# New tables for the order, the engines and the idle products of an mLSTM kernel with a dense layer on one core

## The chip, the cores and the metric

One core of one Trainium2 chip runs the whole program. The metric is the device time of one execution in microseconds (us). Three executions of the kernel before are given, and a profile of one more.

## The reference

The first part is a recurrent attention (mLSTM) over B = 4 sequences, H = 8 heads, 768 steps and a head width of 40, with gates i, f and o. Its result, turned into 3072 tokens of 320 numbers, goes through a dense layer with a softplus between two products:

```
C = f_stab * C + i_stab * outer(v_t, k_t)
n = f_stab * n + i_stab * k_t
y_t = o * (C q_t) / max(|n . q_t|, 1)
...
h = x @ w_in                                   # 320 -> 2048
g = max(h, 0) + log1p(exp(-|h|))
out = g @ w_out                                # 2048 -> 320
```

f_stab and i_stab come from the gates and their running maximum m.

## The kernel before

**Steps and tiles.** A step is 128 time steps of one sequence with all eight heads; it is named by sequence and chunk, and 0_0 is the first chunk of sequence 0. ORDER (line 40) takes the steps 1_0, 2_0, 0_0, then 3_0, 0_1, 0_2 and so on. Three steps make a tile of 384 tokens, and there are eight tiles. The layer can start on a tile when the three steps are done, so tile 0 consists of 1_0, 2_0 and 0_0.

**A step.** `load` (L402, L405) brings q, k and v. `decay` runs a scan on DVE (L432) for the decays pw and a product gw (L437). `plain_scores` multiplies k by q on PE (L483). `by_decays` (L513, DVE) multiplies the scores by the decays. `states` (L500, PE) forms v times k from the scaled values vw (`scaled`, L446 or L450), and `keep_states` copies the result out of PSUM into cp (copy, L789). `values` reads the old states (L599) and the scores (L607) on PE. `sum_values` takes them on DVE (y1z at L446, yy at L628), `norm` forms the denominator nq (L636, L637), `scale_gate` multiplies the out gate og by it (L641), `gated` forms x (L653, on POOL), `turn_x` turns x on PE (L736), and `high_x` and `low_x` (L789, L746) split it into two parts of X. Step states wait for `by_decays` of the same step, because both use one pair of PSUM banks.

**Gates.** `first_gates` (L168 to L198) serves the first chunks, `later_gates` (L208 to L253) the rest: gc at L218 is a subtraction, L220 an exponential, L223, L225 and L226 set up d, and L231 scans. L764 and L768 load and squash the out gates; L843 loads an activation table.

**Weights.** They come as 64-bit words and are made into floats on the chip, in eight slices of w_in (wr, wih, wil) and eight of w_out (wo, woh, wol). `single` has the steps mag (L273 on ACT, L275 elsewhere), the low half (L279), the high half (L283) and a join on DVE into sgi or sgo (L287). `weights` then casts the rounded part into wih (L789) and subtracts it for the remainder (L325 for the wide part wil, L327 for the short third slice); `weights_out` does the same for woh (L789) and wol (L335).

**The layer.** A block is 128 of the 2048 inner columns of one tile: eight products hp (L1003), softplus on ACT (L890, L891), a remainder on DVE (L894), nine products po (L966). The blocks go in the order tile 0 blocks 0 to 9, tile 1 blocks 0 to 15, tile 0 blocks 10 to 15 (SPLIT = 10), then tiles 2 to 7.

**What sets the order.** All work beside the products is a set of generators in a heap. WHEN (L1060) gives each piece of work, by name, a time counted in products of the layer; those below zero come before the first. `tick` runs all pieces due by the current product, `wait_for` runs as many as a product needs, and every engine executes its instructions in the order in which they were recorded. PICK (L1109) names the engine of an elementwise operation: V is DVE, A is ACT, G is POOL; where it has no entry, the default at the call of `pick` holds. WARM (L1108) is the number of identity products that `keep_warm` (L758) puts on PE at eleven places. They write to a corner of PSUM that nobody reads.

```
    def at_of(name, at, base=0):
        return base + WHEN[name] if name in WHEN else at
...
    def pick(name, default):
        return engines[PICK.get(name, default)]
...
    def keep_warm(k):
        for i in range(k):
            nc.tensor.matmul(wm, ident, ident, start=True, stop=True)
```

Of the kernel before, what the change touches and what calls it, by code (L numbers as in the profile page):

```python
# [44 lines left out]
def mlstm_moe_kernel(  # L45
# [20 lines left out]
    p1 = ctx.enter_context(tc.tile_pool(name="p1", bufs=1))  # L66
    p2 = ctx.enter_context(tc.tile_pool(name="p2", bufs=2))
# [692 lines left out]
    og = p2.tile([128, NH, DM], F32, tag="X", bufs=XB, name="og")  # L760
# [296 lines left out]
    def finished(t):  # L1057
        return all(s in ended for s in range(t * NG, (t + 1) * NG))

    WHEN = {'l0': -300, 'p0': -299, 'p1': -298, 'l1': -297, 'p2': -296, 'wl0': -295, 'j0': -294, 'k0': -293, 'p3': -292,  # L1060
# [47 lines left out]
    WARM = {0: 8, 1: 0, 2: 2, 3: 1, 4: 2, 5: 0, 6: 1, 7: 4, 8: 0, 9: 3, 10: 1}  # L1108
# [106 lines left out]
```

## Time and profile before

| what | us |
|---|---|
| three executions | 438.61, 432.89, 437.66 |
| their median | 437.66 |
| the profiled execution | 433.22 |
| its span in the profile | 431.4 |
| PE busy in the span | 419.5 (97%) |
| DVE, ACT, POOL busy | 254.2, 214.7, 106.8 |

Times in the profile count from the start of the span. The profiled execution is 1.8 us longer than its span; that part lies around it. Its granted TensorE clock was 0.991 of full speed on the mean. In the rows, a duration stands behind the start, `x8` is a number of instructions of one kind taken together, and a bracket like [0.56 <-ACT cp] is the time that the engine stood idle before, and what ended it. The operand names drop their buffer numbers. A tile that a step reads under several names (pa, po) is a PSUM bank that was reused.

### The profile page before, as it was taken

How to read it: one execution, taken by the hardware profiler on the slowest of the kernel's cores; microseconds unless marked ns; L12 is line 12 of the kernel's file. 1: busy time of each engine (PE TensorE's matmuls, PEld its weight loads, DVE VectorE, ACT ScalarE, POOL GpSimd, SP SyncE). 2: the span in 40 equal slices, each digit the busy share in tenths (PEclk: the TensorE clock that was granted, in tenths of full speed). 3: DMA queues.
4: the chain of work that ended last, by engine and by line, in shares of the span. 5: the costliest groups of instructions: out<-in, count | busy, mean ns of one | idle time of the engine just before them, and what ended most of it. 6: DMA issues, size and time to landing. Idle time of an engine off the chain costs nothing.

```text
span 431.4 us, 12677 instructions
## 1 busy us (share of the span) xinstructions
PE 419.5 (97%) x5284; PEld 408.0 (95%) x5284; DVE 254.2 (59%) x479; ACT 214.7 (50%) x445; POOL 106.8 (25%) x171
## 2 busy tenths in 40 slices
PE   7769999999999999999999999999999999999996
PEld 7669989999999999999999999999999999999996
DVE  6889998767866646565646556456465555422221
ACT  5688998476455333644336333634236433333332
POOL 3643436444454212212312311222222200000000
PEclk9969999999999999999999999999999999999999
DMA  7888895864655363435273273344363330001001
GB/s 193 265 268 248 252 256 162 248 176 121 157 160 155 117 148 108 130 97 161 67 200 112 64 176 99 112 125 127 98 192 107 71 89 28 2 0 48 0 2 46
DMA packets 52089, 55.93 MB, mean 130 GB/s; under 512 B 5664, under 2 KB 42176, under 8 KB 52032
## 3 DMA queue, kind: packets, MB, share of 16 engines
q1 hardware_dynamic: 49008, 51.68, 43.6%
q10 hardware_dynamic: 3024, 3.44, 2.3%
q8 instruction: 41, 0.67, 0.7%
q14 instruction: 16, 0.13, 0.1%
HBM read 46.47 MB, written 8.64 MB: 128 GB/s over the span
## 4 chain that ended last, share of the span: by engine, by line
PE 93%; DMA 3%; DVE 1%; ACT 1%; POOL 1%; issue 0%; SPq 0%; POOLq 0%; DVEq 0%; ACTq 0%
PE hp L1003 41%; PE po L966 40%; PE hp L483 3%; PE pa L667 2%; PE pa L679 2%; DMA qk<-in_qk 2%; PE hp L500 1%; DMA wr<-in_w_in 1%; PE po L758 1%; PE pa L500 1%; POOL x L653 1%; PE pa L599 1%; PE pa L607 0%; PE pa L483 0%; PE pa L156 0%
## 5 line engine op out<-in xcount | busy, mean ns | idle before, releaser
L1003 PE MATMUL hp<-X,wih 128*128 128x384 f32 x768 | 175.8, 338 | 0.3 <-DVE gl L894 0.3
L890 ACT ACTIVATE gh<-hp 128x384 fp32r<-128x384 f32 x128 | 62.8, 491 | 166.7 <-PE hp L1003 139.0
L894 DVE TENSOR_TENSOR gl<-hp,gh 128x384 fp32r<-128x384 f32 x128 | 70.6, 554 | 123.6 <-ACT hp L891 123.4
L1003 PEld LDWEIGHTS hp<-X,wih 128*128 128x128 f32 x768 | 133.3, 188 | 0.9 <-DVE gl L894 0.6
L966 PE MATMUL po<-woh,gl 128*128 128x320 f32 x384 | 83.2, 313 | 0.0
L966 PE MATMUL po<-wol,gh 128*128 128x320 f32 x384 | 80.8, 310 | 0.0
L966 PE MATMUL po<-woh,gh 128*128 128x320 f32 x384 | 80.7, 310 | 0.1
L966 PEld LDWEIGHTS po<-woh,gh 128*128 128x128 f32 x384 | 65.8, 188 | 0.5 <-ACT woh L789 0.4
L1003 PE MATMUL hp<-X,wil 128*128 128x384 f32 x256 | 65.8, 338 | 0.0
L966 PEld LDWEIGHTS po<-woh,gl 128*128 128x128 f32 x384 | 62.3, 188 | 0.9
L966 PEld LDWEIGHTS po<-wol,gh 128*128 128x128 f32 x384 | 62.0, 188 | 0.6
L891 ACT ACTIVATE hp<-hp 128x384 f32<-128x384 f32 x128 | 62.4, 488 | 0.0
L446 POOL TENSOR_TENSOR vw<-vt,gw 128x328 f32<-128x328 f32 x22 | 17.3, 788 | 118.0 <-DVE gw L437 109.8
L1003 PEld LDWEIGHTS hp<-X,wil 128*128 128x128 f32 x256 | 46.1, 188 | 0.2
L446 POOL TENSOR_TENSOR values_in<-vt,gT 128x328 f32<-128x328 f32 x18 | 13.3, 737 | 65.2 <-PE pa L679 58.6
L432 DVE TENSOR_TENSOR_SCAN pw<-fb,ident 128x512 f32<-128x512 f32 x21 | 26.5, 1263 | 0.0
L578 POOL TENSOR_TENSOR c<-c,cp 104x164 f32<-104x164 f32 x20 | 14.5, 725 | 14.6 <-DMA fc_d<-d 8.2
L713 DVE RECIPROCAL nm<-nm 128x128 f32<-128x128 f32 x18 | 17.2, 953 | 0.6
L511 DVE TENSOR_TENSOR pw<-hp,pw 128x256 f32<-128x256 f32 x36 | 13.6, 419 | 4.6 <-PE hp L500 4.1
L789 ACT COPY cp<-hp 104x164 f32<-104x164 f32 (+1 forms) x31 | 8.2, 283 | 16.2 <-DVE pw L511 14.3
L446 POOL TENSOR_TENSOR c<-c,flast 104x164 f32<-104x164 f32 x33 | 15.5, 470 | 1.0
L569 POOL TENSOR_TENSOR c<-c,cp 104x164 f32<-104x164 f32 x20 | 13.1, 656 | 9.9 <-ACT cp L789 8.2
(162 smaller groups left out, 428.5 us busy)
## 6 DMA issues: line engine op xcount, KB each, us to landing
vt<-in_vk SPq DMA_DIRECT2D x24, 324.0 KB
qk<-in_qk SPq DMA_DIRECT2D x48, 160.0 KB
fb<-fz_d SPq DMA_DIRECT2D x42, 128.0 KB
wo<-in_w_out SPq DMA_DIRECT2D x8, 640.0 KB
wr<-in_w_in SPq DMA_DIRECT2D x8, 512.0 KB
eg<-in_oT SPq DMA_DIRECT2D x6, 576.0 KB
yd<-y SPq DMA_DIRECT2D x36, 96.0 KB
out<-ob ACTq DMA_DIRECT2D x21, 160.0 KB
```

The lines of the kernel that those rows point to most:

```text
L432: nc.vector.tensor_tensor_scan(z.pw.rearrange(flat), z.fb.rearrange(flat), ident4.rearrange(flat), 0.0, ALU.mult, ALU.add)
L446: e.tensor_tensor(to, of, by.unsqueeze(3).broadcast_to([to.shape[0], a, b, w]), op=ALU.mult)
L483: nc.tensor.matmul(z.ga[x][y * Q : (y + 1) * Q, (i * NQ + q) * Q : (i * NQ + q + 1) * Q], z.k[rows, g, ts], z.q[rows, g, ts], start=True, ...
L511: nc.vector.tensor_tensor(pw[:, x], z.ga[x][:, 0:CP0], pw[:, x], op=ALU.mult)
L569: nc.gpsimd.tensor_tensor(heads(z.cm), heads(z.cm), z.cp[:, :, 0], op=ALU.add)
L578: nc.gpsimd.tensor_tensor(heads(c), heads(c), z.cp[:, :, 1], op=ALU.add)
L713: nc.vector.reciprocal(nm, nm)
L890: nc.scalar.activation(gh, hp, AF.Softplus)
L891: nc.scalar.activation(hp, hp, AF.Softplus)
L894: nc.vector.tensor_tensor(gl, hp, gh, op=ALU.subtract)
L966: nc.tensor.matmul(po[j], a[:, j * 128 : (j + 1) * 128], w[:, f, :], start=(first and left[j] == 2), stop=(last and left[j] == 0),)
L1003: nc.tensor.matmul(hp, a, r, start=(i == 0), stop=(i == len(seq) - 1))
```

## The change

Only the three tables change; the code around them is the same, and lines before 1060 keep their numbers.

```diff
-    WHEN = {'l0': -300, 'p0': -299, 'p1': -298, 'l1': -297, 'p2': -296, 'wl0': -295, 'j0': -294, 'k0': -293, 'p3': -292,
...
+    WHEN = {'l0': -314.462812, 'p0': -341, 'p1': -340.5, 'l1': -297.227203, 'p2': -343, 'wl0': -291.469,
...
-    WARM = {0: 8, 1: 0, 2: 2, 3: 1, 4: 2, 5: 0, 6: 1, 7: 4, 8: 0, 9: 3, 10: 1}
+    WARM = {0: 1, 1: 3, 2: 8, 3: 6, 4: 2, 5: 0, 6: 2, 7: 6, 8: 1, 9: 3, 10: 5}
-    PICK = {'wl2': 'V', 'oh6': 'G', 'wl3': 'V', 'mgi7': 'V', 'ol1': 'V', 'ol3': 'V', 'wh5': 'V', 'wi61': 'V', 'ol2': 'V',
...
+    PICK = {'wl2': 'G', 'oh6': 'G', 'wl3': 'G', 'mgi7': 'V', 'ol1': 'V', 'ol3': 'G', 'wh5': 'A', 'wi61': 'A',
...
```

WHEN has 353 entries before and after, with other numbers. The sum of WARM goes from 22 to 37. PICK goes from 68 entries to 185; many of the new ones name the default, 18 of them (sl0_0 to sl0_9, sp0_0 and others) name no operation, and 66 operations change engine: 15 from DVE to POOL, 14 from ACT to DVE, 13 from POOL to DVE, 10 from DVE to ACT, 8 from POOL to ACT and 6 from ACT to POOL. Among them in the first two tiles: the first rounded slice of w_out (oh0) goes from POOL to DVE, the first short remainder of w_in (wm00) from DVE to POOL, the copy of the states of 0_0 (cp2) from DVE to ACT and that of 2_0 (cp1) from ACT to DVE, the later gates' subtraction (gc1) from DVE to POOL, the products of v with the gate or the decay (vi1, vw1, vi2) to DVE and vw3 to ACT, the remainders wl2, wl3 and ol3 from DVE to POOL, and the scaling mgi3 from ACT to POOL.

On PE, the values of 2_0 (written to po2; the operand names end in a buffer's number) stand in the kernel before directly behind the states of 2_0:

```order
L500 MATMUL po2_79<-vw2_0_334,vt2_0_231 64x41
L500 MATMUL po2_79<-vw2_0_334,vt2_0_231 40x41
L599 MATMUL po2_79<-cp2_0_360,qk2_0_228 64x41 x8
L607 MATMUL po2_79<-vi2_0_336,pw2_0_242 64x41 x16
L483 MATMUL pa_75<-qk0_0_289 64x64 x16
L500 MATMUL pa_75<-vw0_0_425,vt0_0_292 64x41
L500 MATMUL pa_75<-vw0_0_425,vt0_0_292 40x41
```

In the changed kernel this place reads:

```order
L500 MATMUL po2_79<-vw2_0_337,vt2_0_216 64x41
L500 MATMUL po2_79<-vw2_0_337,vt2_0_216 40x41
L758 MATMUL po1_80<-ident_82 128x128 x5
L483 MATMUL pa_75<-qk0_0_235 64x64 x16
L599 MATMUL po2_79<-cp2_0_380,qk2_0_213 64x41 x8
L607 MATMUL po2_79<-vi2_0_257,pw2_0_231 64x41 x16
L500 MATMUL pa_75<-vw0_0_365,vt0_0_238 64x41
L500 MATMUL pa_75<-vw0_0_365,vt0_0_238 40x41
```

Five identity products (x5) and the sixteen scores of 0_0 now stand between the states of 2_0 and its values.

On DVE, from the join of the second slice of w_in (sgi1) to the first part of X of tile 0, the rows before are:

```order
L432 SCALAR_TENSOR_TENSOR pw3_0_502<-fb3_0_396,ident4_87 128x512
L437 TENSOR_TENSOR gw3_0_504<-gT_97,pw3_0_502 128x8
L287 SCALAR_TENSOR_TENSOR sgi1_421<-magi1_413,sgi1_421 128x640
L446 TENSOR_TENSOR y1z_99<-po2_79,fcT_98 64x328
L628 TENSOR_TENSOR yy0_0_511<-po2_79,y1z_99 128x2x2x82
L636 SCALAR_TENSOR_TENSOR nq0_0_513<-yy0_0_511 128x8
L637 RECIPROCAL nq0_0_513<-nq0_0_513 128x8
L225 COPY d0_516<-gt0_129 32x4
L226 MEMSET gt0_129 32x4
L641 SCALAR_TENSOR_TENSOR og_127<-nq0_0_513,og_127 128x320
L287 SCALAR_TENSOR_TENSOR sgo0_523<-mago0_521,sgo0_523 128x640
```

And now:

```order
L287 SCALAR_TENSOR_TENSOR sgi1_436<-magi1_393,sgi1_436 128x640
L432 SCALAR_TENSOR_TENSOR pw3_0_485<-fb3_0_370,ident4_87 128x512
L437 TENSOR_TENSOR gw3_0_487<-gT_97,pw3_0_485 128x8
L446 TENSOR_TENSOR y1z_99<-po2_79,fcT_98 64x328
L628 TENSOR_TENSOR yy0_0_518<-po2_79,y1z_99 128x2x2x82
L287 SCALAR_TENSOR_TENSOR sgo0_482<-mago0_472,sgo0_482 128x640
L636 SCALAR_TENSOR_TENSOR nq0_0_521<-yy0_0_518 128x8
L637 RECIPROCAL nq0_0_521<-nq0_0_521 128x8
L789 CAST woh_106<-sgo0_482 128x640
L641 SCALAR_TENSOR_TENSOR og_127<-nq0_0_521,og_127 128x320
L275 TENSOR_SCALAR magi2_569<-wr2_474 128x640
```

The scan for 3_0 with its product now comes behind sgi1; the join of the first slice of w_out (sgo0) and its rounded copy (woh) have moved ahead of the scaled gate (og of nq0_0), and a scaling (magi2) stands behind it.

On POOL, the work on the third and fourth slices of w_in (sgi2, sgi3) and the first states of sequence 0, before:

```order
L789 CAST wih_104<-sgi2_539 128x2x256
L789 CAST wih_104<-sgi2_539 64x128
L327 TENSOR_TENSOR wih_104<-sgi2_539,wih_104 64x128
L578 TENSOR_TENSOR c0_111<-c0_111,cp0_0_463 104x164
L653 TENSOR_TENSOR x3_0_833<-yy3_0_682,sig3_0_649 128x8x48
L446 TENSOR_TENSOR c1_112<-c0_111,flast0_94 104x164
L569 TENSOR_TENSOR c1_112<-c1_112,cp0_1_865 104x164
L789 CAST wih_104<-sgi3_744 128x2x256
```

And now:

```order
L789 CAST wih_104<-sgi2_613 128x2x256
L325 TENSOR_TENSOR wil_105<-sgi2_613,wih_104 128x2x256
L327 TENSOR_TENSOR wih_104<-sgi2_613,wih_104 64x128 x2
L275 TENSOR_SCALAR magi3_754<-wr3_660 128x640
L578 TENSOR_TENSOR c0_111<-c0_111,cp0_0_478 104x164
L653 TENSOR_TENSOR x3_0_807<-yy3_0_701,sig3_0_690 128x8x48
L446 TENSOR_TENSOR values_in_109<-vt0_1_553,gT_97 128x328
L446 TENSOR_TENSOR c1_112<-c0_111,flast0_94 104x164
L569 TENSOR_TENSOR c1_112<-c1_112,cp0_1_871 104x164
L325 TENSOR_TENSOR wil_105<-sgi3_804,wih_104 128x2x256
L327 TENSOR_TENSOR wih_104<-sgi3_804,wih_104 64x128 x2
```

Wide and short remainders of both slices (L325, L327), a scaling (magi3) and a product with v (values_in) have come to this place, and the cast of the wide part of the fourth slice has left it.

## Rows read from the trace of the kernel before

**Rows 1.** Stretches: length, busy us of each engine (instructions), clock, DMA share, GB/s.

```profile
core 0: us, PE busy (x) PEld busy (x) DVE busy (x) ACT busy (x) POOL busy (x), PEclk, DMA share, GB/s
...
10.00:20.00 10.00, 7.87 (x230) 6.80 (x222) 8.84 (x15) 5.36 (x10) 6.82 (x9) 1.00 0.92 273
20.00:30.00 10.00, 6.70 (x147) 6.16 (x140) 8.29 (x20) 8.55 (x19) 3.27 (x5) 0.69 0.93 275
30.00:40.00 10.00, 9.34 (x163) 8.08 (x163) 9.28 (x17) 8.45 (x14) 5.75 (x8) 0.96 0.76 225
40.00:50.00 10.00, 10.00 (x140) 9.50 (x139) 9.46 (x24) 9.35 (x21) 3.16 (x6) 1.00 0.87 255
```

**Rows 2.** Waits of PE from 40 to 110 us: total, times, longest.

```profile
PE hp L1003 <- DVE gl L894: 0.3, 1, 0.3
```

**Rows 3.** Order of time, 14 to 34 us: start, length, instruction, idle before.

```profile
16.95 1.16 PE L758 MATMUL po<-ident 128*128 128x128 f32 x8
...
17.84 0.74 POOL L446 TENSOR_TENSOR vw<-vt,gw 128x328 f32<-128x328 f32 x1 [1.69 <-DMA vt<-in_vk]
...
19.27 0.49 PE L599 MATMUL po<-cp,qk 40*64 40x41 f32 x10 [0.56 <-ACT cp L789]
...
20.51 0.50 DVE L446 TENSOR_TENSOR y1z<-po,fcT 64x328 f32<-64x328 f32 x1 [1.06 <-PE po L607]
...
21.90 0.78 ACT L273 ACTIVATE magi<-wr 128x640 f32<-128x640 f32 x1 [0.40 <-DMA wr<-in_w_in]
...
22.74 0.21 PE L483 MATMUL pa<-qk 40*64 40x64 f32 x1 [1.86 <-issue]
22.99 0.69 DVE L513 TENSOR_TENSOR pw<-pa,pw 128x512 f32<-128x512 f32 x1 [0.47 <-PE pa L483]
...
27.47 0.50 DVE L446 TENSOR_TENSOR y1z<-po,fcT 64x328 f32<-64x328 f32 x1
...
29.09 0.48 DVE L641 SCALAR_TENSOR_TENSOR og<-nq,og 128x320 f32<-128x320 f32 x1
...
31.66 0.69 PE L483 MATMUL pa<-qk 40*64 40x64 f32 x32
...
32.72 0.96 PE L1003 MATMUL hp<-X,wih 128*128 128x384 f32 x4
```

**Rows 4.** DVE from its first scan to the last part of X.

```profile
8.64:32.92 24.28, 21.21 (x43) 0.86 0.91 267
```

**Rows 5.** DVE's groups by form, 8 to 33 us: busy, mean ns, idle.

```profile
L432 DVE TENSOR_TENSOR_SCAN pw<-hp,ident 128x512 f32<-128x512 f32 x3 | 3.6, 1201 | 0.0
...
L287 DVE SCALAR_TENSOR_TENSOR sgo<-mago,sgo 128x640 uint32<-128x640 uint32 x1 | 0.8, 818 | 0.0
...
L789 DVE COPY cp<-pa 104x328 f32<-104x328 f32 x1 | 0.5, 500 | 0.3 <-PE pa L500 0.3
L327 DVE TENSOR_TENSOR wih<-sgi,wih 64x128 fp32r<-64x128 f32 x1 | 0.3, 284 | 0.0
```

**Rows 6.** Groups by form, whole span: DVE, ACT, POOL.

```profile
L218 DVE TENSOR_TENSOR gt<-gt,m 32x768 f32<-32x768 f32 x1 | 0.9, 937 | 0.0
...
L789 DVE CAST woh<-sgo 128x640 fp32r<-128x640 f32 x1 | 0.5, 488 | 0.0
...
L843 ACT ACT_TABLE_LOAD x2 | 2.6, 1283 | 0.0
...
L275 POOL TENSOR_SCALAR mago<-wo 128x640 f32<-128x640 f32 x1 | 2.4, 2429 | 0.0
...
L325 POOL TENSOR_TENSOR wil<-sgi,wih 128x512 fp32r<-128x512 f32 x1 | 1.4, 1357 | 1.6 <-DVE wih L789 1.6
```

**Rows 7.** DMA queues: transfers, MB, share of 16 engines.

```profile
q8 instruction: 41, 0.67, 0.7%
```

**Rows 8.** Order of time, 68 to 71 us, POOL and DVE.

```profile
68.12 1.59 POOL L335 TENSOR_TENSOR wol<-sgo,woh 128x640 fp32r<-128x640 f32 x1
...
68.57 2.21 DVE L432 TENSOR_TENSOR_SCAN pw<-fb,ident 128x512 f32<-128x512 f32 x1
```

140 rows, old and new, of tables (PICK, WHEN) are left out of this document.

## The prediction, made blind

> **What bounds the kernel now.** Three views in this order: the stretches with each engine's busy time, the waits of TensorE, and the order of time in the front. The stretches [rows 1] show two regimes. From 10 to 30 us TensorE (PE) is busy 7.87 and 6.70 us of 10, and over the second of these at a granted clock of 0.69. From 30 on it is busy 9.34, from 40 on 10.00. The waits say the same: from 40 to 110 us PE waits once, 0.3 us, for VectorE (DVE) [rows 2]. Behind 33 us the two large products therefore set the time, and nothing done on DVE, ScalarE (ACT) or GpSimd (POOL) there can gain more than that 0.3 us. What can be gained lies before the first product of the layer, which starts at 32.72 us [rows 3].
>
> What holds that start is the third step of the first tile, 0_0. In the order of time [rows 3] its scores end on PE at 22.95, DVE multiplies by the decays at 22.99, and when its states and values have gone over PE, DVE takes them at 27.47 (y1z) and has the scaled gate ready at 29.57 (29.09 + 0.48). POOL's product x, PE's turning of it and the parts of X follow, and behind the scores and states of the next step the first product starts. Beside this chain DVE is busy 21.21 of the 24.28 us from its first scan (8.64) to the last part of X (32.92) [rows 4], and from 30 to 50 some 9.3 to 9.5 of every 10 [rows 1]. So DVE is the engine whose order counts, and it has 3.07 us of idle time in the front.
>
> **The change, part by part.** The sum is made against the profiled execution: 433.22 us for a span of 431.4.
>
> *Loads.* The gates come first, wih's second slice before the first of w_out; the bytes ahead of step 0_0 are the same. POOL still waited for that step's values until 17.84 [rows 3]. I cost this at nothing. Its cover is that DVE and PE reach step 0_0 some microseconds after 17.84; an order that reached it at 17 would show the load again. The first scan can start up to 0.6 us earlier (one copy and the waiting for the later gates stand before it no longer), but PE meets step 1_0's values again behind a copy on ACT, now queued behind one more conversion: nothing gained, 0.3 at best.
>
> *PE between the values of 1_0 and of 2_0.* Before: four identity products (eight records, 1.16 us, so 0.29 for one), states, then values of 2_0 at 19.27 behind a wait of 0.56 for a copy [rows 3]. Now: six identity products, states, five more, the scores of 0_0, then the values of 2_0. Added: 2 x 0.29 = 0.58, 5 x 0.29 = 1.45, and the scores, 0.69, as the same product of the next step shows at 31.66 [rows 3]. The wait of 0.56 goes, since that copy runs on DVE beside the five. 0.58 + 1.45 + 0.69 - 0.56 = 2.16, so DVE's y1z for 2_0, which waited for PE at 20.51, starts at 22.67.
>
> *DVE from there to the gate of 0_0.* Before, 20.51 to 29.57 is 9.06 us, of which 0.5 (at 22.99 [rows 3]) and 0.3 (before the copy [rows 5]) are waits for PE. The change takes out of this piece the multiplication by the decays (0.69 [rows 3]), one remainder (0.28) and a copy (0.50) [rows 5], and puts in the join of the first w_out slice (0.82) [rows 5] and its rounded copy (0.49) [rows 6], both ahead of the gate of 0_0: +1.31 - 1.47 = -0.16. The waits go, as PE has passed everything by then: ACT's copy of the states of 0_0 now stands behind three conversions and a table load, from the landing of the second w_in slice at 21.90 [rows 3]. Three conversions of 0.78 and the load of 1.28 [rows 6] are 3.6, so the copy starts at about 25.5 at the latest and the values follow within some 1.5 us, by 27.0; DVE, 2.16 later but without the waits and the 1.47, comes to them at 27.47 + 2.16 - 0.8 - 1.47 = 27.4. That cover is thin, 0.4 us; were the conversions longer by more, y1z would wait for the rest. 9.06 - 0.8 - 0.16 = 8.10, so the gate is ready at 22.67 + 8.10 = 30.77, 1.2 us later than 29.57. The rest to the first product (29.57 to 32.72, 3.15 us) keeps its operations and engines. The first product starts at 33.9.
>
> *From there to 40 us.* PE's idle time in 30 to 40 is 0.66 us [rows 1]; the blocks of the first products are cut differently around the gates and step 3_0. I let half of it be given back, an estimate with the ends 0 and 0.66: -0.3.
>
> *The added load on the engines.* In all, 66 operations change engine. On DVE in the front seven come (three products with v, two casts, a copy and a scaling of wide tiles), counted at the 0.49 of w_out's cast [rows 6]: 3.4 us. Four go: the later gates' subtraction (0.94) [rows 6], the short remainder (0.28), a cast of its size (0.28 too) and a copy (0.50): 2.0. That is +1.4. This is in the sum above as far as it stands on the path. Two more table loads on ACT, 2.6 us, lie in ACT's idle time (10 - 5.36 and 10 - 8.55 in the stretches from 10 to 30 [rows 1]) except for the one counted above. Fifteen more identity products than before, 4.4 us of PE, are harmless except for the seven counted: the other groups end while PE waits for a load or for x.
>
> *From 33 to 69 us.* DVE is relieved of about 0.8 us of work (two wide remainders and a scaling go to POOL, less what comes from ACT, an estimate by the rows 5 and 6), and POOL gains eight (rival 3). I take 0: before, DVE waited for PE at the end of this stretch, and PE had no more than the 0.3 us to give [rows 2]. The ends are -0.3 and +4.3. I cost the new order behind 69 us at nothing; the cover is PE's unbroken row of products.
>
> Sum: +1.2 - 0.3 = **+0.9 us**, say +1.0 with 0.1 for the rounding of a chain of twenty instructions. In the profiled execution that is 434.2 us. The three runs shown are at 432.89, 437.66 and 438.61, so the profiled one stands 4.4 below their median; carried to the median the forecast is 437.66 + 1.0 = **438.7 us**.
>
> **A rule weighed against a row.** At 22.74 PE idles 1.86 us with nothing to wait for in the profile [rows 3]: one matmul of 32, then the next step's. The 16 DMA engines are at 93% of their time [rows 1], and the instruction queue moves 0.67 MB in 41 transfers [rows 7], about 16 KB each: this reads as PE waiting for its own code. The Trainium skill, Runtime: NRT & Kernel Launch, section Instruction fetch mechanics, says that crossing a 16 KiB block of code is mostly hidden. Here the row disagrees by 1.86 us, if that is what it is; by the rule it would be a wait of another kind and no reason for a rival.
>
> **Rivals.**
>
> 1. *DVE's idle time closes* (faster). If the reordering lets DVE run on without waits from its first scan, 0.6 us earlier, its 21.21 + 1.4 = 22.6 us of work end X at 8.04 + 22.6 = 30.7 instead of 32.92: -2.2, so 435.5. For it: DVE has 3.07 idle in the front and its work is what counts. Against: the identity products stand on PE between DVE's operations.
>
> 2. *The code wait returns* (slower). Ten more identity products (two records each) and the scores of 0_0 stand ahead of the values of 2_0, so the same block of code ends inside the values of 2_0. Before, the 1.86 us cost only 0.47, DVE's wait at 22.99. Now DVE's y1z waits for exactly that: +1.0 + 1.9 = +2.9, so 440.6. Against: it was seen once.
>
> 3. *POOL stands in DVE's way from 33 to 69 us* (slower). POOL gets two wide remainders of w_in (1.36 each) and a scaling (2.43) [rows 6], one remainder of w_out (1.59) [rows 8], two short remainders and a product with v, less a cast; these last counted net as two halves of a wide remainder: 2.72 + 2.43 + 1.59 + 1.36 = 8.1 us. At 68.57 a scan on DVE took 2.21 instead of the 1.20 of its like at the start [rows 5] while POOL's 1.59 us remainder ran [rows 8]; 1.0 over 1.59 is 0.63 us lost for each of POOL's. At that rate DVE loses 5.1 us in a stretch where it has hardly any idle time, less the 0.8 it is relieved of: +4.3 on top of the 438.7, so 443.0. It decides from the point where DVE no longer catches up with PE before X of the second tile (69 us); if every one of POOL's 8.1 us were lost to DVE, the time would be 446.8, 2.1% above the median. Against: before, too, POOL was busy 3.16 of 10 us beside a DVE busy 9.46 [rows 1], and PE waited for nothing; and POOL can be the one that waits.
> The Trainium skill, SBUF — State Buffer, section Who interferes with whom, calls this an exclusive lock: a DVE instruction with two SBUF inputs and a GpSimd one that reads SBUF block each other for the whole instruction. The trace agrees in that one scan.
>
> That the change does not do what it says holds in part: 18 names in the table of engines belong to no operation of this kernel.
>
> **How the numbers follow.** Forecast 0.47; rival 1 0.25, rival 2 0.13, rival 3 0.15. The range takes the lowest run shown with rival 1 (432.89 - 2.2 = 430.7) and the highest with rival 3's price (438.61 + 4.3 = 442.9). A difference under 2% (8.8 us) is about what a measurement of this kernel can't tell from none. Faster by more would need the first product at 24 us, and DVE's work alone from 8.04 on lasts to 30.7: 0.01. Slower by more is the far end of rival 3: 0.04. Within 2%: 0.95.
>
> **What would show it.** Right: the first product near 33.9; y1z of 2_0 near 22.7 waiting for PE; two operations on w_out between yy and the gate of 0_0; PE without waits behind 40. Rival 1: DVE idle under 1 us in the front, first product before 31.5. Rival 2: PE idle over 1 us before y1z of 2_0 with no releaser. Rival 3: scans and remainders on DVE well over 1.3 us and PE waiting for DVE between 50 and 70. The forecast is wrong as a whole if PE waits for ACT or POOL behind 70, or if the first product moves and the end does not.

## The result, and the profile after

| | kernel before | changed kernel |
|---|---|---|
| median, us | 435.47 (432.0 to 438.77, 20 runs) | 437.62 (435.21 to 439.44, 20 runs) |
| ratio to before, 95% interval | | 1.0054 (1.0031 to 1.0078) |
| profiled execution, us (span) | 433.22 (431.4) | 436.57 (434.6) |
| first product of the layer, us | 32.72 | 33.05 |
| from there to the end of the span, us | 398.68 | 401.55 |

The ratio is 2.4 us at the median of before. The last two rows split the two profiled spans: +0.33 us in the front and +2.87 us behind it. The forecast was +1.0 us, laid wholly in the front.

Behind the front, the waits of PE from 40 us to the end, in the changed kernel (the one row of [rows 2] answers to its last one):

```profile
PE pa L483 <- ACT gT L247: 1.0, 1, 1.0
PE pa L736 <- DVE cp L789: 0.8, 1, 0.8
PE pa L599 <- POOL c L569: 0.6, 1, 0.6
PE pa L483 <- DVE yy L628: 0.4, 1, 0.4
PE hp L1003 <- DVE gl L894: 0.2, 1, 0.2
```

Four waits are new, on three engines, 2.8 us in all. They make up nearly all of the 2.87 us. The stretches of the changed kernel, which answer to [rows 1], show the same (columns as there; PE busy is the second number):

```profile
20.00:30.00 10.00, 6.89 (x163) 6.57 (x155) 9.61 (x21) 8.38 (x18) 5.35 (x5) 0.83 0.97 265
30.00:40.00 10.00, 8.73 (x161) 7.58 (x160) 9.61 (x20) 8.53 (x15) 6.82 (x8) 1.00 0.80 232
40.00:50.00 10.00, 9.04 (x130) 8.24 (x129) 7.88 (x17) 6.90 (x15) 6.61 (x7) 1.00 0.78 231
...
60.00:70.00 10.00, 8.59 (x110) 7.94 (x109) 8.17 (x18) 7.89 (x20) 6.51 (x6) 1.00 0.79 240
```

Where PE was busy 10.00 of 10 before, it is now busy 9.04. POOL has doubled from 3.16 to 6.61, and DVE, which the prediction took for the engine to watch, has fallen from 9.46 to 7.88: it waits too.

The front in order of time, to set beside [rows 3] (start, length, instruction, idle before):

```profile
14.96 0.49 PE L599 MATMUL pa<-cp,qk 40*64 40x41 f32 x10
...
17.55 0.67 PE L500 MATMUL po<-vw,vt 64*64 64x41 f32 x32
18.15 1.38 PE L758 MATMUL po<-ident 128*128 128x128 f32 x10
...
19.23 0.45 DVE L789 COPY cp<-po 104x328 f32<-104x328 f32 x1
...
19.46 0.69 PE L483 MATMUL pa<-qk 40*64 40x64 f32 x32
...
19.99 0.44 PE L599 MATMUL po<-cp,qk 40*64 40x41 f32 x10
...
21.12 0.50 DVE L446 TENSOR_TENSOR y1z<-po,fcT 64x328 f32<-64x328 f32 x1
...
23.82 0.43 ACT L789 COPY cp<-pa 104x328 f32<-104x328 f32 x1
...
24.46 1.46 POOL L653 TENSOR_TENSOR x<-yy,og 128x384 f32<-128x384 f32 x1
...
25.03 1.96 DVE L432 TENSOR_TENSOR_SCAN pw<-fb,ident 128x512 f32<-128x512 f32 x1
...
27.23 0.50 DVE L446 TENSOR_TENSOR y1z<-po,fcT 64x328 f32<-64x328 f32 x1
...
28.34 0.82 DVE L287 SCALAR_TENSOR_TENSOR sgo<-mago,sgo 128x640 uint32<-128x640 uint32 x1
...
29.40 0.44 DVE L789 CAST woh<-sgo 128x640 fp32r<-128x640 f32 x1
...
29.76 0.48 DVE L641 SCALAR_TENSOR_TENSOR og<-nq,og 128x320 f32<-128x320 f32 x1
...
33.05 0.96 PE L1003 MATMUL hp<-X,wih 128*128 128x384 f32 x4
```

The row at 14.96 is the values of 1_0, which in the kernel before start 0.93 us later:

```profile
15.89 0.49 PE L599 MATMUL pa<-cp,qk 40*64 40x41 f32 x10
```

PE runs the states of 2_0 (17.55), the five identity products (ten records, 18.15 to 19.53) and the scores without a wait, and the values of 2_0 start at 19.99. The copy of the states that these values read, on DVE from 19.23 to 19.68, was done by then. y1z of 2_0 comes at 21.12, not at the forecast 22.67. Then DVE needs 9.12 us to the end of the scaled gate (30.24), not 8.10: its scan took 1.96 us beside POOL's x, and a small copy (L225, 22.56) took 0.69 us beside POOL's scaling of w_out, where it had taken 0.11 before.

### The profile page after: what moved, and what is told of

Same layout as the page of the kernel before. It is cut to its first block, busy times and chain, and to the rows that moved or that the text cites. A ratio compares the mean times of both kernels' runs of the same rounds, so it can differ in the third digit from the quotient of the medians.

```text
span 434.6 us, 12740 instructions
## 1 busy us (share of the span) xinstructions
PE 420.9 (97%) x5314; PEld 409.7 (94%) x5314; DVE 261.0 (60%) x480; ACT 211.7 (49%) x441; POOL 118.3 (27%) x173
## 3 DMA queue, kind: packets, MB, share of 16 engines
HBM read 46.47 MB, written 8.64 MB: 127 GB/s over the span
## 4 chain that ended last, share of the span: by engine, by line
PE 87%; DVE 3%; DMA 3%; issue 2%; SPq 2%; POOL 2%; ACT 1%; DVEq 0%; ACTq 0%; POOLq 0%
PE hp L1003 39%; PE po L966 38%; PE hp L483 3%; PE pa L667 2%; PE pa L679 2%; PE hp L500 1%; DMA wr<-in_w_in 1%; DMA qk<-in_qk 1%; DVE pw L432 1%; DMA flast<-fl_d 1%; POOL x L653 1%; PE po L758 1%; PE pa L483 1%; SPq L402 1%; POOL c L446 0%
## 5 line engine op out<-in xcount | busy, mean ns | idle before, releaser
L446 POOL TENSOR_TENSOR vw<-vt,gw 128x328 f32<-128x328 f32 x21 | 15.5, 737 | 117.9 <-DVE gw L437 109.8
L446 POOL TENSOR_TENSOR values_in<-vt,gT 128x328 f32<-128x328 f32 x19 | 15.1, 792 | 64.6 <-PE pa L679 64.5
L432 DVE TENSOR_TENSOR_SCAN pw<-fb,ident 128x512 f32<-128x512 f32 x21 | 27.9, 1329 | 0.0
L446 POOL TENSOR_TENSOR c<-c,flast 104x164 f32<-104x164 f32 x34 | 18.5, 545 | 1.2
L569 POOL TENSOR_TENSOR c<-c,cp 104x164 f32<-104x164 f32 x20 | 15.7, 783 | 9.4 <-ACT cp L789 8.1
L686 DVE TENSOR_TENSOR y<-pa,y 112x512 f32<-112x512 f32 x18 | 12.4, 689 | 5.0 <-PE po L966 2.7
```

Source lines behind the costliest of these rows:

```text
L432: nc.vector.tensor_tensor_scan(z.pw.rearrange(flat), z.fb.rearrange(flat), ident4.rearrange(flat), 0.0, ALU.mult, ALU.add)
L446: e.tensor_tensor(to, of, by.unsqueeze(3).broadcast_to([to.shape[0], a, b, w]), op=ALU.mult)
L569: nc.gpsimd.tensor_tensor(heads(z.cm), heads(z.cm), z.cp[:, :, 0], op=ALU.add)
L686: nc.vector.tensor_tensor(y2, z.gc[0 : PP + EP, :, 0:CP0], y2, op=ALU.mult)
```

## The experiments

The table has every run. "First" is the start of the first product of the layer in its profile, "rest" the span from there to the end, "waits" PE's waits from 40 us on.

| run | median, us | ratio to before (95%) | first | rest | waits |
|---|---|---|---|---|---|
| before | | | 32.72 | 398.68 | 0.3 |
| changed | 437.62 | 1.0054 (1.0031 to 1.0078) | 33.05 | 401.55 | 3.0 |
| e1 old identity products | 439.17 | 1.0081 (1.0050 to 1.0112) | 36.16 | 400.74 | 1.4 |
| e2 old engines | 446.36 | 1.0261 (1.0220 to 1.0301) | 33.17 | 411.33 | 7.9 |
| e3 before, new engines | 443.39 | 1.0174 (1.0129 to 1.0219) | 34.09 | 407.11 | 4.2 |
| e4 before, new identity products | 436.91 | 1.0033 (1.0007 to 1.0059) | 37.24 | 398.66 | 0.3 |
| e5 POOL relieved | 438.66 | 1.0072 (1.0041 to 1.0104) | 33.51 | 402.49 | 1.6 |
| e6 same order again | 436.04 | 1.0004 (0.9974 to 1.0033) | 32.85 | 400.15 | 1.6 |
| e7 turn and states moved | 437.85 | 1.0035 (1.0008 to 1.0061) | 34.12 | 401.88 | 2.9 |
| e9 five identity products out | 438.77 | 1.0055 (1.0025 to 1.0085) | 34.71 | 401.59 | 2.8 |
| e10 conversion behind gates | 436.21 | 1.0022 (0.9992 to 1.0051) | 32.98 | 400.92 | 2.2 |
| e11 scores before join | 438.28 | 1.0055 (1.0030 to 1.0081) | 32.71 | 402.39 | 3.9 |
| e12 w_out behind X | 438.95 | 1.0054 (1.0026 to 1.0082) | 32.49 | 404.31 | 1.0 |
| e13 new front, old rest | 435.80 | 1.0018 (0.9985 to 1.0052) | 33.02 | 399.48 | 0.8 |

The rest goes with the waits: 398.68 at 0.3 us, 400.15 at 1.6, 400.92 at 2.2, 401.55 at 3.0, 402.39 at 3.9. Where it lies more than 2 us above that line, PE also ran at a lower granted clock behind its waits: 0.83 from 50 to 60 us and 0.57 from 80 to 84 in e2, 0.74 from 70 to 80 in e3; e5 and e12 are shown below. "First", "rest" and "waits" stand on one profiled execution of each kernel.

### The three tables apart

**e1.** `WARM` of before in the changed kernel.

```diff
-    WARM = {0: 1, 1: 3, 2: 8, 3: 6, 4: 2, 5: 0, 6: 2, 7: 6, 8: 1, 9: 3, 10: 5}
+    WARM = {0: 8, 1: 0, 2: 2, 3: 1, 4: 2, 5: 0, 6: 1, 7: 4, 8: 0, 9: 3, 10: 1}
```

> The changed kernel with the old numbers of identity products (WARM sum 22 instead of 37), order and engines as changed. Theory 1 (the loss arises between 40 and 70 us, where PE waits 2.8 us in four places, and the front gives only 0.3): the time stays within 0.5 us of the changed kernel's, so 1.5 to 2.5 us above the kernel before. Theory 2 (the prediction's: identity products on PE in the front push the values of 2_0 and with them the first product): 1.0 to 2.0 us faster than the changed kernel, so within 1 us of the kernel before, and the first product 1 us earlier than 33.05.

Measured 439.17, that is 1.6 us above the changed kernel by the medians and 1.2 by the ratios, no more than two comparisons of one program can differ by (e6); the first product of the profile starts 3.1 us later. Neither theory had the sign. Fewer identity products don't help.

**e4.** The other way round, in the kernel before.

```diff
-    WARM = {0: 8, 1: 0, 2: 2, 3: 1, 4: 2, 5: 0, 6: 1, 7: 4, 8: 0, 9: 3, 10: 1}
+    WARM = {0: 1, 1: 3, 2: 8, 3: 6, 4: 2, 5: 0, 6: 2, 7: 6, 8: 1, 9: 3, 10: 5}
```

> The kernel before with the new numbers of identity products alone (fifteen more). Theory 2 (they push the front): 1 to 2 us slower, the first product at 33.7 to 34.7 instead of 32.72. Theory 1: within 0.5 us of the kernel before.

436.91, a ratio of 1.0033, or 1.4 us: slower, as theory 2 has it. In the profiled execution (437.94) the first product starts at 37.24, far behind theory 2's 34.7, and the rest is that of before to 0.02 us: in this profile the identity products act on the front alone. But they don't act as theory 2 says. The places differ between the two orders, and both e1 and e4 have only two and one identity products at the very start, where their kernels have eight. The first decays on PE (32 records of L416) then run slower, as the order of time shows for the kernel before, the changed kernel and e1:

```profile
5.95 2.38 PE L416 MATMUL hp<-g,ident 128*64 128x128 f32 x32
```

```profile
5.29 1.97 PE L416 MATMUL hp<-g,ident 128*64 128x128 f32 x32
```

```profile
5.02 3.68 PE L416 MATMUL hp<-g,ident 128*64 128x128 f32 x32 [2.11 <-DVE m L211]
```

In e4 the row is 3.68 too. Identity products at the start are worth some 1.3 to 1.7 us to the row behind them; the prediction counted them as a cost alone.

Nor does it end with that row. The second group of decays (16 records of L416) is still slow in e4 and no longer in e1, two microseconds later:

```profile
12.65 1.80 PE L416 MATMUL hp<-g,ident 128*64 128x128 f32 x16
```

```profile
14.85 1.09 PE L416 MATMUL hp<-g,ident 128*64 128x128 f32 x16
```

The trace's list of granted clocks agrees with this. Its first entry, each time of 1.00, starts at 5.10 us in the changed kernel, 6.83 before, 14.43 in e1 and 14.14 in e4; ahead of it there is no entry, and a stretch without one is printed as 1.00. So PE most likely ran at the lower of its two levels up to that time (no entry says it; a slow row takes 1.6 to 1.9 times as long as its like behind the first entry). In the two kernels with eight products PE worked from 1.69 us on almost without a break; in e1 and e4 it stood idle for over 2 us behind its two and one.

**e2.** `PICK` of before in the changed kernel; order and identity products stay.

```diff
-    PICK = {'wl2': 'G', 'oh6': 'G', 'wl3': 'G', 'mgi7': 'V', 'ol1': 'V', 'ol3': 'G', 'wh5': 'A', 'wi61': 'A',
...
+    PICK = {'wl2': 'V', 'oh6': 'G', 'wl3': 'V', 'mgi7': 'V', 'ol1': 'V', 'ol3': 'V', 'wh5': 'V', 'wi61': 'V', 'ol2': 'V',
...
```

> The changed order and identity products, but every operation on the engine that it had before. Theory 3 (POOL's extra work is what makes PE wait between 40 and 70 us): POOL is busy under 5 us of every 10 there instead of 6.6, PE's four waits of 2.8 us together fall under 1 us, and the time goes back to within 0.7 us of the kernel before. Theory 4 (the new order alone does it: a conversion that waits for its DMA stands on ACT ahead of the gates' copy): the wait of 1.0 us before the scores at 45 us stays, and the time stays 1.5 to 2.5 us above the kernel before.

446.36, 9 us above the changed kernel. Theory 3 is off altogether, and theory 4 is far too small. PE's longest wait comes at 78.70, for a cast of w_out that now stands on POOL:

```profile
78.70 0.71 PE L966 MATMUL po<-woh,gh 128*128 128x320 f32 x3 [2.83 <-POOL woh L789]
```

**e3.** `PICK` of the changed kernel in the kernel before (the diff of e2 the other way).

> The kernel before with the new table of engines alone. Theory 3 (POOL's extra work): PE waits 2 us or more between 40 and 70 us, and the time is 2 to 3 us above the kernel before. Theory 4 (the order): PE waits under 1 us there, and the time is within 1 us of the kernel before.

443.39, 7.7 us above before. The new engines alone cost 7.7 us, the new order with new identity products and old engines (e2) 10.7 us, and all of them together 2.2 us by the medians. The tables fit each other; the parts of such a change have no price of their own that could be added up. A sum of edits, each priced against the old order, can't see that.

### Where the loss is, and what makes it

**e13.** The split: up to the first product the changed kernel's tables, behind it those of the kernel before. The order on each engine is that of the changed kernel to about 33 us, and from there on that of before.

```diff
-        'cp3': 1.57585, 'gc3': 9.0938, 'scan4': 12.54685, 'w2_1_1': 28.823913, 'ga5': 104.291
+        'cp3': 2.667, 'gc3': 11.333, 'scan4': 15.25, 'w2_1_1': 49.333, 'ga5': 104.167
...
-        'wl2': 'G', 'wl3': 'G', 'ol3': 'G', 'mgi3': 'G'
+        'wl2': 'V', 'wl3': 'V', 'ol3': 'V'
...
```

> The changed kernel's order, engines and identity products for all that stands before the first product of the layer, and the order and engines of the kernel before for all that comes later. Theory 8 (the loss lies wholly in the new order and engines behind the first product, and the new front costs nothing): the first product starts within 0.6 us of 33.05, the time from there to the end is 398.3 to 399.2 us as in the kernel before (398.68) instead of 401.55, PE has no wait over 0.4 us behind 40 us, and the time is 2 to 3 us below the changed kernel: 0 to 1.2 us below the kernel before. Theory 9 (the old rest fits only the old front): PE waits 1 us or more between 40 and 70 us, and the time is at or above the changed kernel's.

The first product starts at 33.02 and the rest is 399.48: 2.07 of the 2.87 us are gone, and the time can't be told from that of the kernel before (1.0018, from 0.9985 to 1.0052). By the time alone that would show nothing, as e6 below, with the changed kernel's own order, stands at 1.0004; it is the rest in the profile that shows it. Theory 9 falls. Theory 8 holds in its main part; the rest is 0.3 us above its range, with this row of waits behind 40 us:

```profile
PE hp L1003 <- DVE gl L894: 0.8, 2, 0.5
```

So most of the loss in the profiles lies in the new order and engines behind 33 us, and the new front costs next to nothing, but gains nothing either.

**e5.** Is it POOL's extra work? Five operations go back.

```diff
-    'wl2': 'G', 'wl3': 'G', 'ol3': 'G', 'mgi3': 'G', 'vi4': 'G'
+    'wl2': 'V', 'wl3': 'V', 'ol3': 'V', 'mgi3': 'A', 'vi4': 'A'
```

> The changed kernel with five operations taken off POOL and back to the engines of before (the wide remainders of the third and fourth w_in slices and the remainder of the fourth w_out slice to DVE, the scaling of the fourth w_in slice and one product of v to ACT; some 8 us of POOL). Theory 3 (POOL's extra work stands in DVE's way and makes PE wait): PE's waits behind 40 us fall from 3.0 to under 1.5 us, and the time is 1 to 2 us below the changed kernel. Theory 5 (order and engines fit each other, and DVE and ACT have no room for this work where it now stands): PE's waits behind 40 us stay or grow, and the time is the changed kernel's or up to 4 us above.

The waits fall from 3.0 to 1.6, nearly as theory 3 has it, but the time is 438.66, 1 us above the changed kernel, as theory 5 has it. ACT now makes PE wait for its product with v (0.86 and 0.56 us), and behind that PE runs at half its clock. Three stretches of e5 (columns: stretch, length, PE busy, granted clock, DMA share, GB/s):

```profile
54.00:56.00 2.00, 0.58 (x25) 1.00 0.82 249
56.00:58.00 2.00, 2.00 (x31) 0.73 0.16 52
58.00:60.00 2.00, 2.00 (x8) 0.50 0.37 35
```

At 0.50, the lower of the two levels (1.2 GHz), 2 us of PE do the work of 1.

**e6.** One entry of the order.

```diff
-        'w1_1_0': 11.864425
+        'w1_1_0': 13.2
```

> The changed kernel with one entry of the order changed: the first conversion of the second w_out slice on ACT, which waited 1.95 us for its transfer, comes behind the later gates' copy instead of ahead of it. Theory 4 (that order makes PE wait at 45 us): the wait of 1.0 us before the scores there goes, nothing takes its place, and the time from the first product to the end falls by 0.7 to 1.0 us. Theory 3: the wait stays or its time comes back in another wait behind it, and the time from the first product to the end stays within 0.3 us of 401.55.

The edit moved the wrong entry: the conversion ahead of the gates' copy is that of the third w_out slice (w2_1), and with this one the order on all engines is the changed kernel's. So e6 says nothing of theory 4, but it is a second measurement of the changed kernel: 436.04 against 437.62, a ratio of 1.0004 against 1.0054. And in its profile the wait for the gates' copy is not there, because the transfer that the conversion waits for landed 1.3 us earlier (the conversion, L273 on ACT, starts at 42.95 there). In the kernel before the copy (L247) stood ahead of that conversion, as ACT's order of time shows, first before, then the changed kernel:

```profile
43.16 0.22 ACT L247 COPY gT<-pa 128x96 f32<-128x96 f32 x1
...
44.87 0.77 ACT L273 ACTIVATE mago<-wo 128x640 f32<-128x640 f32 x1
```

```profile
44.30 0.78 ACT L273 ACTIVATE mago<-wo 128x640 f32<-128x640 f32 x1 [1.95 <-DMA wo<-in_w_out]
...
44.99 0.22 ACT L247 COPY gT<-pa 128x96 f32<-128x96 f32 x1
```

This wait comes and goes with a DMA: it is 0.9 to 1.5 us in e7, e9 and e11 and absent in e1, e5 and e12, and none of these edits touches it. And two comparisons of the same program can differ by 0.5%, so no smaller difference between two ratios of the table is evidence for a cause; what the runs show of causes is in their profiles.

**e10.** The same with the right entry.

```diff
-        'w2_1_1': 28.823913
+        'w2_1_1': 30.5
```

> The changed kernel with one entry of the order changed: on ACT the first conversion of the third w_out slice (mago2), which waits for its transfer, stands behind the later gates' copy (gT, L247) instead of ahead of it. Theory 4 (the order makes PE wait at 45 us): PE has no wait for that copy any more, and the time from the first product to the end is 400.2 to 400.7 us (401.55 in the profile of the changed kernel, 400.15 in one whose transfer came early). Theory 7 (the wait only moves, to the weights that this conversion feeds): a wait of 0.5 us or more for woh, wih or the join turns up behind 45 us, and the time from the first product to the end stays above 401 us.

PE's wait for the gates' copy is gone, and the rest falls by 0.63 us to 400.92, 0.2 above the range of theory 4 since the wait for yy on DVE rose to 0.6. Its time (436.21) can't be told from e6's. Theory 7 falls.

**e7.** Two moves to take away the waits at 62 and 66 us.

```diff
-        'xp4': 110.122934, 'xh4': 112.195, 'w4_0_5': 96.964444
+        'xp4': 113.3, 'xh4': 113.4, 'w4_0_5': 122.6
```

> The changed kernel with two places of the order changed: the turning of x of step 0_1 comes three products later on PE, and the remainders of the fifth w_in slice come behind the state sum (L569) that the values of step 0_2 wait for on POOL. Theory 4 (the order makes these waits): both waits (0.8 and 0.6 us) go, and the time from the first product to the end falls by 1.0 to 1.4 us. Theory 3 (POOL and DVE are too full there, whatever the order): the state sum ends no more than 0.3 us earlier, or the waits come back at the next step, and less than 0.5 us is gained.

Nothing gained (rest 401.88). The edit also put the join of that slice behind the next step's scores, since a slice's conversions take their entries in order of time. The wait for the state sum went, the wait for cp grew to 1.0 us, and two new ones of 0.4 us came, for wih and wil. By the expectation this is theory 3's "the waits come back"; the next run asks it with a cleaner order.

**e11.** Join behind the decays, the copy on ACT, the short remainders on DVE.

```diff
-        'w4_0_5': 96.964444, 'pm5': 110.122594, 'cp5': 110.122651
+        'w4_0_5': 108.0, 'pm5': 104.35, 'cp5': 104.4
-        'cp5': 'V', 'wm40': 'G', 'wm41': 'G'
+        'cp5': 'A', 'wm40': 'V', 'wm41': 'V'
```

> The changed kernel with DVE's and POOL's order changed around 60 us only: the join of the fifth w_in slice comes behind the decays of step 0_2, that step's copy of the states goes from DVE to ACT, and the two short remainders of the slice go from POOL to DVE. Theory 4 (order): the waits of 0.8 us before the turning of x and of 0.6 us before the values of 0_2 both fall under 0.2 us, and the time from the first product to the end falls by 0.9 to 1.4 us against the changed kernel. Theory 3 (POOL and DVE get in each other's way whatever the order): one of the two waits stays above 0.4 us.

The waits of PE from 40 us on in e11:

```profile
PE pa L599 <- DVE X L746: 1.5, 1, 1.5
PE pa L483 <- ACT gT L247: 1.5, 1, 1.5
...
PE pa L736 <- ACT cp L789: 0.3, 1, 0.3
```

The wait for cp falls to 0.3 and that for the state sum goes, but the work that left POOL stands on DVE ahead of X, and the values of 0_2 now wait 1.5 us for that. The rest is 402.39, 0.84 above the changed kernel's; 0.5 of that is the gates' copy, which the edit doesn't touch. Neither theory had this: the wait changes its engine.

### Two terms of the front

**e9.** The five identity products between states and values of 2_0 left out (`WARM[1]` 3 to 0, `WARM[6]` 2 to 0).

```diff
-    1: 3, 6: 2
+    1: 0, 6: 0
```

> The changed kernel without the five identity products between the states and the values of step 2_0. The prediction's sum: they stand on the path, so the first product starts 1.4 us earlier (31.6) and the time falls by 1 to 1.5 us. Theory 6 (PE waits for the copy of the states there anyway, which DVE ends at 19.7): the values start within 0.3 us of 19.99, the first product within 0.5 us of 33.05, and the time stays within 0.7 us of the changed kernel.

The values start at 19.97 instead of 19.99, within the 0.3 us of theory 6. But that agreement is partly chance, since in this profile the states of 2_0 start 1.12 us later than in the changed kernel (17.55):

```profile
18.67 0.61 PE L500 MATMUL po<-vw,vt 64*64 64x41 f32 x30
...
19.97 0.49 PE L599 MATMUL po<-cp,qk 40*64 40x41 f32 x10
```

From the states to the values it is 1.30 us here and 2.44 there. DVE's copy ended at 19.91 here, 0.06 before the values; in the changed kernel it ended at 19.68, so without the five the values could have started some 0.25 us before 19.99 there (an estimate from these two rows). The five stand on PE's path, and the copy would have taken nearly all of their place. Inside the values PE then stood still for 2.03 us with nothing to wait for, and the first product of that execution came 1.66 us later than the changed kernel's; by the ratios the time is the changed kernel's (1.0055 against 1.0054). The order of time of e9:

```profile
22.95 0.37 PE L607 MATMUL po<-vi,pw 64*64 64x41 f32 x10 [2.03 <-issue]
23.41 0.50 DVE L446 TENSOR_TENSOR y1z<-po,fcT 64x328 f32<-64x328 f32 x1 [2.09 <-PE po L607]
```

This is the mechanism of rival 2. Counted from 3 us on, 345 matmul records of PE stand before this stop in e9. In e7 it is 345 too, before the same operation, and in the kernel before and in e3 345 again, before another one, the scores of 0_0 (the rows of e7 and e3):

```profile
21.95 0.49 PE L607 MATMUL po<-vi,pw 64*64 64x41 f32 x19 [0.37 <-issue]
```

```profile
23.05 0.21 PE L483 MATMUL pa<-qk 40*64 40x64 f32 x1 [1.23 <-issue]
```

So it belongs to a place in PE's program and not to an operation, and it lasts 0 to 2.03 us, the changed kernel's profile showing none. In e7 and e9 a shorter one (0.39 and 0.69 us) stands 127 records earlier. The Trainium skill, Runtime: NRT & Kernel Launch, section Instruction fetch mechanics, tells of code that each engine's sequencer fetches in blocks of 256 instructions while it runs, at a cost that is "mostly hidden". The distance of 127 records agrees with that: with the weight loads and the rows of PE's sequencer counted in, the two stops of e7 and e9 stand 449 and 705 rows into the trace, 256 apart. The 2.03 us are not hidden.

The trace's list of transfers shows what PE waits for. On the instruction queue (q8) 41 or 42 transfers of 16 KB go to some 10,650 rows of PE, one for every 256 or so. In e9 the first two end at 15.22 and 21.45, and PE goes on 1.55 and 1.50 us behind these ends (16.77 and 22.95). At row 705 it goes on 1.71, 1.39 and 1.48 us behind the end of the second transfer in the kernel before, e3 and e7. In the ten other kernels, the changed one among them (its transfer ended at 18.02, the row came at 20.46), that end lay 1.5 to 2.4 us ahead of the row, and PE didn't stop there. So the stop is PE waiting for its code, whenever the transfer comes late; why it comes late is not shown.

**e12.** The join and rounded copy of the first w_out slice behind X of tile 0.

```diff
-        'w0_1_0': -208.419282, 'w0_1_5': -200.841914, 'w0_1_4': -194.97857
+        'w0_1_0': -182.9, 'w0_1_5': -182.8, 'w0_1_4': -182.7
```

> The changed kernel with the join and the rounded copy of the first w_out slice on DVE behind the last part of X of tile 0 instead of ahead of the scaled gate of step 0_0. The prediction's term (1.31 us of these two stand on the path to the gate and with it to the first product): the gate of 0_0 comes 1.2 to 1.5 us earlier against y1z of the same step, the first product starts 0.7 to 1.3 us earlier in respect of that y1z, and nothing waits for this slice later. Rival (PE's other work or POOL's product x holds the start): the first product keeps its distance of 5.8 us from that y1z.

The scaled gate starts 1.59 us behind y1z (27.33 to 28.92) instead of 2.53, so 0.94 of the 1.31 us were on that path, less than the theory's 1.2. The first product comes 5.16 us behind y1z instead of 5.82: 0.66 us of it arrives. Then it is lost with interest. PE waits 0.84 us for ACT's copy of the next step's states and 0.76 us for DVE's gate scan, and its clock is halved behind that (columns as in e5):

```profile
34.00:36.00 2.00, 0.97 (x12) 1.00 0.61 164
36.00:38.00 2.00, 1.43 (x12) 0.72 1.02 386
38.00:40.00 2.00, 2.00 (x44) 0.50 0.79 166
40.00:42.00 2.00, 2.00 (x21) 0.50 0.93 285
42.00:44.00 2.00, 2.00 (x9) 0.57 0.94 285
```

The missing shares of these stretches are 0.28, 0.50, 0.50 and 0.43 of 2 us each, 3.4 us in all.

The rest is 404.31, and the ratio is the changed kernel's.

## Why the prediction came out as it did

The forecast for the time was right: +1.0 us was forecast, the ratio says +2.4 (1.3 to 3.4), e6 some 0.2 for the same order, and all of it lies within 2% and in the range. The reason given was wrong in place: terms of the front were missed in opposite directions, and the term that was set at nothing holds nearly all of the loss. That the sum fell near is in part luck, and so is the nearness of 438.7 to the measured 437.62: the base, a median of three runs, was 2.2 us above that of twenty.

- *"Loads": "nothing gained, 0.3 at best".* Failed: the first scan started at 7.70 instead of 8.64, and the copy on ACT behind which PE was to meet the values of 1_0 again came earlier too (14.49 instead of 15.39), so these values started at 14.96 instead of 15.89. That is 0.93 us gained.
- *"PE between the values of 1_0 and of 2_0", +2.16 us.* The place was right, the size not: from the values of 1_0 to y1z of 2_0 it took 6.16 us instead of 4.62, +1.54. The scores and the identity products overlap on PE, so that a row's duration counts more than it adds: the five added 1.31 and the scores 0.53, where 1.45 and 0.69 were counted. With the 0.93 from above, y1z of 2_0 came 0.61 us later (21.12 against 20.51). Not seen was a second releaser close behind: DVE's copy of the states ended only at 19.68, since DVE was busy until 19.23, so leaving the five out could have given back some 0.25 us there, not their 1.45 (e9).
- *"DVE from there to the gate of 0_0", 8.10 us.* Failed the other way: 9.12. The operations were the right ones (e12 took 0.94 us back), but the durations were taken from before. The scan took 1.96 instead of 1.20 while POOL's x ran beside it from 24.46 to 25.92, and the copy L225 0.69 instead of 0.11. From its first scan to the last part of X, DVE was busy 24.55 of 25.52 us; before it was 21.21 of 24.28 [rows 4]. That is +3.3 of work where +1.4 was counted.
- *The first product at 33.9.* It started at 33.05: 1.55 early by y1z, 1.02 late by the piece behind it, and 0.34 early since from the gate to the first product it took 2.81 us instead of 3.15. The cover of ACT's copy held: it started at 23.82, and 25.5 at the latest was forecast.
- *"From there to 40 us", -0.3.* A misread row: in both kernels this idle time lies ahead of the first product, as a wait for POOL's x (first before, then changed), so that there was nothing behind it to give back.

```profile
31.18 0.55 PE L736 MATMUL hp<-ident,x 128*128 128x128 f32 x3 [0.65 <-POOL x L653]
```

```profile
31.51 0.55 PE L736 MATMUL hp<-ident,x 128*128 128x128 f32 x3 [1.23 <-POOL x L653]
```

- *"From 33 to 69 us ... I take 0".* The step that failed most: four new waits, +2.87 us (e13 takes 2.07 of it back). The argument was that PE had been kept busy before and that DVE would get less work. But a wait is made by one instruction that stands behind another on its engine: the gates' copy behind a conversion that waits for a DMA (ACT), cp behind the decays and gl (DVE), the state sum behind two remainders (POOL), yy behind a scan (DVE). The sum of an engine's work says nothing of that; the order of the instructions, known before any run, shows where such a wait can arise, though not how long it is or whether a transfer comes late.
- *Rival 1.* DVE's idle time did close, from 3.07 to 0.97 us, and bought nothing, as its work grew by more.
- *Rival 2.* The stop is real, moves to where the rival put it, and costs what was said (2.03 us in e9). In the profile of the changed kernel it is absent, because there the code had landed 2.4 us ahead (18.02 against 20.46). The reading of the row as a wait for code was right; what the prediction had no term for is when that transfer comes.
- *Rival 3.* Right in its stretch, wrong in its victim. POOL got 10.3 us (24.1 against 13.9 busy from 33 to 70), near the forecast 8.1 and some stretching. Yet DVE's scans are not longer there (1378 ns in the mean of two, 1550 in the mean of three before); its joins of w_out are, a little (987 against 839). POOL's own operations are, by far. Groups on POOL from 33 to 70 us, first the kernel before, then the changed one:

```profile
L446 POOL TENSOR_TENSOR c<-c,flast 104x164 f32<-104x164 f32 x3 | 1.4, 462 | 0.1
L569 POOL TENSOR_TENSOR c<-c,cp 104x164 f32<-104x164 f32 x2 | 1.0, 506 | 0.2
```

```profile
L446 POOL TENSOR_TENSOR c<-c,flast 104x164 f32<-104x164 f32 x3 | 3.6, 1206 | 0.1
...
L569 POOL TENSOR_TENSOR c<-c,cp 104x164 f32<-104x164 f32 x2 | 2.0, 1021 | 0.7 <-DVE cp L789 0.6
```

The same scaling of the states goes from 462 to 1206 ns, and the sum behind it from 506 to 1021. That chain is one of the four waits (0.6 us). e5 shows that it isn't the whole: with POOL relieved the time stays.

What stays open: how much of the 2.4 us is the program and how much the draw of its transfers. e6 and the first comparison have the same order of instructions and differ by 0.5%. The split into front and rest stands on one profile of each kernel; in those that leave the changed front as it is, the first product starts between 32.71 and 34.12. A version that beats both was not found; e13 equals the kernel before.

## What to carry to other kernels

In a kernel whose engines are all nearly full, price a new order by places, not by sums: for each instruction that PE waits for, look what now stands ahead of it on its own engine, and whether that one waits for a transfer. An operation counts on the path only if nothing else releases the next one later, so look for the other releaser before adding it. Tables of order and of engines that were set together are tested together: the new engines alone were 7.7 us slower here, the new order with the old engines 10.7, and both together 2.2.

## What the runs showed that was not expected

- The stop of PE without a releaser stands 705 rows of PE into the trace in four kernels, whatever operation stands there, and lasts from 0.37 to 2.03 us. PE goes on 1.4 to 1.7 us behind the end of a 16 KB transfer on the instruction queue; where that transfer had landed 1.5 us or more before the row, there is no stop.
- In e5 and e12, and in e2 and e3, PE's granted clock went to 0.50 (1.2 GHz) behind its waits. In e12 waits of 1.6 us were followed by 3.4 us lost to the clock: a wait can be paid more than twice.
- The first decays took 1.97 us behind eight identity products and 3.68 behind two. The granted clock is printed as 1.00 for both, but for the second the trace has no clock entry there: its first one starts at 14.43 us, that of the changed kernel at 5.10. A printed 1.00 at the start of a span is worth something only together with the durations of the rows.
